# Fetching eight residual tiles one by one inside the down products, behind the LayerNorm transposes

## Chip, cores and metric

One Trainium2 chip, one core of it. The metric is the device time of one execution in microseconds (us). A few other words used below: PE is the matmul engine (TensorE), DVE is VectorE, ACT is ScalarE, POOL is GpSimd, and SP is SyncE, which does no arithmetic here and issues the DMAs in the order of its program.

## The reference

Four layers on `x` of 2048 tokens by 1024 channels in bf16: linear attention (A), a bilinear feed-forward layer (B), and the same two again, each behind a LayerNorm and with a residual.

```python
x = A_x
x = x + _A_ref(_layernorm(x), A_wqkv, A_wo)
x = x + _B_ref(_layernorm(x), B_w_gate, B_w_up, B_w_down)
x = x + _A_ref(_layernorm(x), A_wqkv, A_wo)
x = x + _B_ref(_layernorm(x), B_w_gate, B_w_up, B_w_down)

def _B_ref(x, w_gate, w_up, w_down):          # F = 3584
    g = x @ w_gate ; u = x @ w_up
    return (g * u) @ w_down
```

## The kernel before

Layer B handles its tokens in two halves (`ps_` 0 and 1, 1024 tokens each). Each half has a gate-up stage and a down stage. The down stage is a Strassen-like scheme of seven products, taken in the order 1, 2, 6, 7, 4, 5, 3; the first four have four steps (`t`) of 14 matmuls each. Everything is recorded operation by operation, with the dependences found from byte ranges, and the order in which the program records is the order on each engine. All DMAs but none of the arithmetic go on SP:

```python
def dma(dst_ap, src_ap, wr, key, rd=()):
    P.add("sp", lambda e: e.dma_start(dst_ap, src_ap), rd=rd, wr=wr, dma_sem=key)
```

During the gate-up stage the SBUF space of eight tiles of the residual `x` (128 tokens by 1024, 256 KB each) is lent to scratch. The tiles wait in a DRAM copy (`x_scratch`) and are fetched back when the gate-up stage ends. That is in the last part of its tail, which runs inside the first step of the first down product:

```python
def tail(part):                    # ... parts 0 to 2 end the gate-up stage ...
    for _ in range(2 if "R1" not in order else 1):
        ring_issue()               # weights of the down products, ~0.9 MB each
    for t in range(8 if l2 and not jit else 0):
        i = 8 * ps_ + t
        dma(x_res[:, i, :], xscr[i * 128:(i + 1) * 128, :], r_x(i), KX[i], rd=R(V_X + i * 32, 32))
```

So it happens in three of the four halves; the first half of the first layer lends nothing (`jit`). I call them the first, second and third place. The residual is read where a product is evacuated, that is, read out of PSUM and worked into the output: tiles 0 to 3 of the half first in product 2, tiles 4 to 7 first in product 7:

```python
def evac(t, q=q):                  # after the matmuls of step t of product q
    ...
    elif q in "24":
        xs, rx = xq(sh, 0, t)      # left half of residual tile 4*sh + t
        stt(xs, pb, CD, a, ra_, rx, prd=[bank])
    ...
    ticks(q, t)                    # other work slipped in: LayerNorm steps, stores
    l2_ops(q, t)                   # DVE sums for later products
```

`ticks` carries LayerNorm work. In the second place it is the last four token tiles of this layer's own LayerNorm, needed by the second half. One step hands the previous tile to a DMA transpose on SP, writes the next normalized tile on DVE, and starts the statistics of one more:

```python
def flush_step(self):
    self.step_t(1)                 # SP: dma_start_transpose(xnT[...], xn[n % 2])
    ...
    self.b2_one()                  # DVE: xn[n % 2] = (x - mean) * rstd      (L496)
    ...
    self.start(self.n)             # DVE, POOL: statistics of the next tile
```

For these last tiles there are two buffers `xn`. The write of tile n + 2 has to wait until the transpose of tile n has read its buffer.

## Time and profile before

| | before |
|---|---|
| three runs known to the prediction, median (range), us | 1430.34 (1430.0 to 1430.77) |
| profiled execution, span, us (its device time) | 1429.3 (1431.05) |
| PE busy | 1421.5 us (99 %) |
| DVE busy | 1205.5 us (84 %) |
| second place, from the unbroken row of its first product to the next gate-up stage | 1107.01 to 1186.82 us: 79.81 us |

The prediction shows the page's header, the chain that ended last, and the waits. Two more views of the second place carry the argument. In the timeline of SP (start, length, line, operation, destination<-source, number of DMAs) the eight residual loads stand ahead of the first three transposes, and two weight loads behind those:

```profile
1107.59 4.39 SPq L428 DMA_DIRECT2D arena<-x_scratch  x8
1112.33 10.51 SPq L579 DMA_TRANSPOSE arena<-arena  x3
1122.89 1.06 SPq L428 DMA_DIRECT2D arena<-t_scratch  x2
```

In the timeline of DVE the bracket at the end of a line gives the idle time ahead of it and what ended that:

```profile
1112.57 2.17 DVE L806 TENSOR_TENSOR arena<-arena 128x1792 f16<-128x1792 f16 x2
1121.04 0.55 DVE L496 TENSOR_SCALAR arena<-arena 128x1024 f16<-128x1024 bf16 x1 [6.31 <-DMA arena<-arena]
```

DVE has nothing it may do from 1114.7 to 1121.0, because the buffer that L496 writes is held by the first transpose.

### The profile page before, as it was taken

How to read it: one execution, taken by the hardware profiler on the slowest of the kernel's cores; microseconds unless marked ns; L12 is line 12 of the kernel's file. 1: busy time of each engine (PE TensorE's matmuls, PEld its weight loads, DVE VectorE, ACT ScalarE, POOL GpSimd, SP SyncE). 2: the span in 40 equal slices, each digit the busy share in tenths (PEclk: the TensorE clock that was granted, in tenths of full speed). 3: DMA queues.
4: the chain of work that ended last, by engine and by line, in shares of the span. 5: the costliest groups of instructions: out<-in, count | busy, mean ns of one | idle time of the engine just before them, and what ended most of it. 6: DMA issues, size and time to landing. Idle time of an engine off the chain costs nothing.

```text
span 1429.3 us, 21974 instructions
## 1 busy us (share of the span) xinstructions
PE 1421.5 (99%) x8209; PEld 790.0 (55%) x8209; DVE 1205.5 (84%) x2356; ACT 712.5 (50%) x1455; POOL 154.5 (11%) x193
## 2 busy tenths in 40 slices
PE   9999999999999999999999999999999999999999
PEld 4444444555546566664554444456666475666548
DVE  7897978999888799987689978888888787888888
ACT  5882355444410266655377714567775004777400
POOL 3203521000010000002010045300000100000000
PEclk9999999999999999999999999999999999999999
DMA  7868979997786776769784366767775976777653
GB/s 237 222 142 221 217 177 203 300 316 265 251 263 211 239 255 243 257 222 303 230 280 104 101 173 167 167 197 259 245 255 197 273 255 231 257 263 254 208 194 122
DMA packets 270699, 320.74 MB, mean 224 GB/s; under 512 B 164096, under 2 KB 211072, under 8 KB 270592
## 3 DMA queue, kind: packets, MB, share of 16 engines
q1 hardware_dynamic: 270592, 319.34, 73.1%
q8 instruction: 64, 1.05, 0.3%
q14 instruction: 43, 0.35, 0.1%
HBM read 236.45 MB, written 73.40 MB: 217 GB/s over the span
## 4 chain that ended last, share of the span: by engine, by line
PE 86%; DVE 7%; issue 2%; ACT 2%; POOL 1%; DMA 1%; SPq 0%; POOLq 0%; DVEq 0%
PE ps L1419 28%; PE ps L1502 17%; PE ps L1854 13%; PE ps L1235 8%; PE ps L974 8%; PE ps L1761 6%; PE ps L1337 4%; DVE arena L806 3%; DVE arena L455 2%; PE ps L947 1%; DMA arena<-arena 1%; DVE arena L809 1%; POOL arena L466 1%; PE ps L1261 1%; PE ps L1288 0%
## 5 line engine op out<-in xcount | busy, mean ns | idle before, releaser
L806 DVE TENSOR_TENSOR arena<-arena 128x512 f16<-128x512 f16 (+7 forms) x1027 | 507.2, 522 | 57.2 <-ACT arena L1506 32.7
L1419 PE MATMUL ps<-arena 128*128 128x512 f16 x1888 | 457.1, 379 | 0.5 <-DVE arena L809 0.4
L809 DVE SCALAR_TENSOR_TENSOR arena<-ps,arena 128x512 f16<-128x512 f32 (+3 forms) x558 | 358.4, 658 | 76.8 <-PE ps L1854 36.8
L1502 PE MATMUL ps<-arena 128*128 128x256 f16 x2184 | 287.5, 273 | 0.0
L1419 PEld LDWEIGHTS ps<-arena 128*128 128x128 f16 (+1 forms) x1888 | 182.6, 98 | 163.2 <-ACT ps L1448 3.8
L1502 PEld LDWEIGHTS ps<-arena 128*128 128x128 f16 (+1 forms) x2184 | 211.9, 98 | 90.6 <-ACT arena L1506 6.9
L1854 PE MATMUL ps<-arena 128*128 128x512 bf16 (+1 forms) x1064 | 232.6, 379 | 1.7 <-DVE arena L806 1.7
L1854 PEld LDWEIGHTS ps<-arena 128*128 128x128 f16 x1064 | 103.8, 98 | 125.9 <-DVE arena L806 2.2
L1424 ACT ACTIVATE arena<-ps 128x512 f32<-128x512 f32 x224 | 133.7, 597 | 76.8 <-PE ps L1419 62.9
L1506 ACT ACTIVATE arena<-ps 128x256 f32<-128x256 f32 x351 | 125.1, 384 | 26.4 <-PE ps L1502 21.5
L974 PE MATMUL ps<-arena 128*128 128x512 f16 (+1 forms) x616 | 134.7, 380 | 0.6 <-ACT arena L981 0.6
L1235 PE MATMUL ps<-arena 128*128 128x512 bf16 x512 | 116.1, 379 | 0.0
L1337 PE MATMUL ps<-arena 128*128 128x512 bf16 x512 | 110.8, 379 | 0.0
L1512 ACT COPY ps<-ps 128x256 f32<-128x256 f32 x182 | 66.4, 365 | 75.3 <-DVE arena L809 28.6
L974 PEld LDWEIGHTS ps<-arena 128*128 128x128 f16 x616 | 59.3, 98 | 74.9 <-ACT arena L981 5.8
L1761 PE MATMUL ps<-arena 128*128 128x256 f16 (+1 forms) x882 | 97.2, 273 | 0.5 <-DVE arena L809 0.5
L1448 ACT COPY ps<-ps 128x512 f32<-128x512 f32 x112 | 65.4, 584 | 62.2 <-PE ps L1419 51.9
L1076 POOL TENSOR_TENSOR arena<-arena 128x1024 f16<-128x1024 f32 x32 | 76.2, 2381 | 156.7 <-DVE arena L1074 141.2
L1761 PEld LDWEIGHTS ps<-arena 128*128 128x128 f16 x882 | 86.0, 98 | 11.9 <-DVE arena L809 1.0
L1515 DVE TENSOR_TENSOR ps<-ps,arena 128x256 f32<-128x256 f32 x182 | 76.7, 428 | 10.6 <-PE ps L1502 9.6
L1337 PEld LDWEIGHTS ps<-arena 128*128 128x128 f16 x512 | 50.0, 98 | 60.5
L1789 ACT COPY arena<-ps 128x256 f32<-128x256 f32 x8 | 3.0, 372 | 158.3 <-PE ps L1761 158.3
(72 smaller groups left out, 980.5 us busy)
## 6 DMA issues: line engine op xcount, KB each, us to landing
arena<-w_scratch SPq DMA_DIRECT2D x84, 896.0 KB, 4.5
arena<-t_scratch SPq DMA_DIRECT2D x32, 896.0 KB, 6.0
arena<-in_B_w_down_dram SPq DMA_DIRECT2D x24, 896.0 KB, 5.2
arena<-sp_scratch SPq DMA_DIRECT2D x26, 768.0 KB, 4.2
w_scratch<-arena SPq DMA_DIRECT2D x28, 512.0 KB, 6.2
arena<-w_scratch SPq DMA_DIRECT2D x28, 384.0 KB, 5.1
x_scratch<-arena SPq DMA_DIRECT2D x40, 256.0 KB, 5.0
arena<-x_scratch SPq DMA_DIRECT2D x40, 256.0 KB, 6.1
```

What stands on the lines that cost most here:

```text
L806: P.add("dve", lambda e: e.tensor_tensor(out=out, in0=a, in1=b, op=op), rd=rd, wr=wr, prd=prd)
L809: P.add("dve", lambda e: e.scalar_tensor_tensor(out=out, in0=a, scalar=sc, in1=b, op0=ALU.mult, op1=op1), rd=rd, wr=wr, prd=prd)
L974: P.add("pe", lambda e: [e.matmul(psb(bank), a[0][:, k, :], b[0][:, k, :], start=(q in (1, 5) and k == 0), stop=(k == 3), skip_group_check ...
L1235: return [e.matmul(psb(bank), xrt[t][:, jj * 128:(jj + 1) * 128], pk[:, h, t, :], start=(t == tok[0]), stop=(t == tok[NST - 1])) for t in ts]
L1337: return [e.matmul(psb(bank), xnT[:, g, i * 128:(i + 1) * 128], wp[:, g, dh * 512:(dh + 1) * 512], start=(dh == 0 and g == 0), stop=(g == ...
L1419: P.add("pe", lambda e: [e.matmul(psb(bank), w[:, k, :], x[:, k, :], start=(start and k == 0), stop=(k == 3), skip_group_check=True) for k ...
L1424: P.add("act", lambda e: e.activation(t, psb(bank), AF.Copy, scale=SG), prd=[bank], wr=r)
L1502: P.add("pe", lambda e: [e.matmul(psb(bank)[:, 256 * half:256 * half + 256], w[:, k, :], xx[:, k, :], start=(start and k == 0), stop=(k == ...
L1506: P.add("act", lambda e: e.activation(d, src, AF.Copy, scale=sc), prd=[xk], wr=rd_)
L1515: P.add("dve", lambda e: e.tensor_tensor(out=half(c, 1), in0=U, in1=c5, op=ALU.add), prd=[xk], rd=rc5, pwr=[dst[c]])
L1761: P.add("pe", lambda e: [e.matmul(psb(bank)[:, 256 * half:256 * half + 256], a[:, k, 128 * r:128 * r + 128], b[:, k, :], start=(start and ...
L1854: P.add("pe", lambda e: [e.matmul(psb(bank), hv[:, 7 * hf + k, t * 128:(t + 1) * 128], w[:, k, :], start=(q in "15" and hf == 0 and k == 0 ...
```

## The change

The intent is to take the eight loads from ahead of the transposes and give each to a step one or two products ahead of its use: tiles 0 to 3 behind the `ticks` of product 1 (used in product 2), tiles 4 to 7 behind those of product 2 (used in product 7, the fourth).

```diff
                     for _ in range(2 if "R1" not in order else 1):
                         ring_issue()
-                    for t in range(8 if l2 and not jit else 0):
-                        i = 8 * ps_ + t
-                        dma(x_res[:, i, :], xscr[i * 128:(i + 1) * 128, :], r_x(i), KX[i], rd=R(V_X + i * 32, 32))
                 return tail
@@ evac @@
                         ticks(q, t)
+                        if q in "12" and (ps_ or not first):
+                            i = i0 + 4 * "12".index(q) + t
+                            dma(x_res[:, i, :], xscr[i * 128:(i + 1) * 128, :], r_x(i), KX[i], rd=R(V_X + i * 32, 32))
                         l2_ops(q, t)
```

## The prediction

> **What bounds the kernel now.** I read the page's header, then the chain that ended last, then the waits and the engines' timelines of the one stretch the chain pointed to.
>
> ```profile
> span 1429.3 us, 21974 instructions
> PE 1421.5 (99%) x8209; PEld 790.0 (55%) x8209; DVE 1205.5 (84%) x2356; ACT 712.5 (50%) x1455; POOL 154.5 (11%) x193
> ```
>
> TensorE (PE) is busy for all but 1429.3 - 1421.5 = 7.8 us. That is a hint only, since the ends of matmuls are modelled, so I take the pitch of matmuls from unbroken rows of the chain: 259 of 128x512 in 55.90 us are 0.2158 us each, 196 of 128x256 in 21.40 us are 0.1092 us each. Where matmuls follow each other at this pitch, no moved transfer can gain anything. The change touches three places, the heads of three of the four down stages, near 649, 1107 and 1351 us. Of the first and the third the chain says:
>
> ```profile
> 648.85 55.90 PE ps L1854 x259
> 704.75 21.40 PE ps L1761 x196
> ...
> 1350.65 43.81 PE ps L1854 x203
> 1394.46 29.82 PE ps L1761 x273
> ```
>
> The columns are start and length. Both places run at the pitch without a break (203 x 0.2158 = 43.8; 273 x 0.1092 = 29.8): nothing is to be had there. At the second, which is the first down stage of the second bilinear layer, the chain leaves PE and goes through the DMA queue:
>
> ```profile
> 1106.29 0.90 PE ps L1419 x4
> ...
> 1107.59 0.43 SPq L428
> ...
> 1111.54 0.44 SPq L428
> 1111.98 0.35 issue
> 1112.33 8.61 DMA arena<-arena
> ```
>
> The L428 rows from 1107.59 to 1111.98 are the issues of the eight residual loads (256 KB each). The last row is the first LayerNorm transpose, an SBUF-to-SBUF DMA that stood behind them and took 8.61 us to land; the median over the 60 transposes of this line is 4.0 us. The waits of this stretch say who paid:
>
> ```profile
> DVE arena L496 <- DMA arena<-arena: 6.3, 1, 6.3
> ...
> PE ps L1854 <- DVE arena L806: 1.7, 1, 1.7
> ...
> PE ps L1761 <- DVE arena L809: 0.5, 1, 0.5
> ```
>
> VectorE (DVE) stood still once, 6.3 us, because its next LayerNorm output (L496) writes one of two buffers and the late transpose was still reading that one. From there DVE works with a backlog, and later PE waits for DVE twice. The timeline of PE shows where:
>
> ```profile
> 1107.01 31.89 PE L1854 MATMUL ps<-arena 128*128 128x512 bf16 x147
> 1140.57 12.26 PE L1854 MATMUL ps<-arena 128*128 128x512 f16 x56 [1.66 <-DVE arena L806]
> 1152.66 3.98 PE L1761 MATMUL ps<-arena 128*128 128x256 f16 x35
> 1157.15 17.75 PE L1761 MATMUL ps<-arena 128*128 128x256 f16 x161 [0.50 <-DVE arena L809]
> ```
>
> Start to start: 147 x 0.2158 = 31.73, so the fourth product could start at 1138.74 and starts at 1140.57: 1.83 us lost. 56 x 0.2158 leads to 1152.66, as seen. 35 x 0.1092 = 3.82 leads to 1156.48, and the next starts at 1157.15: 0.67 us lost. Together 2.50 us in this stage; after 1157.15 the rows join again.
>
> **What the Trainium skill says.** (1) "DMA: Bandwidth & Descriptors", section "Queues, rings and completion order": on each DMA engine descriptors are consumed in ring order, and SP owns one row of rings. All these transfers are issued from SP, so bytes issued earlier are moved earlier; the 8.61 us against 4.0 agree. (2) The same page, "Anatomy of one DMA": DMA engines do not wait on semaphores, the issuing sequencer does, before it dispatches. So one blocked issue on SP holds all that follow. The queue's own waits in this stretch agree: it waits 3.3 and 3.9 us ahead of two transposes whose source DVE had not written, and the two weight loads behind them went out only at 1122.89. (3) "TensorE: Matmul & The Clock Gate", section "Wait — 56ns, not 53.3ns?": back-to-back matmuls of N = 512 are 215.7 ns apart once warm. The trace has 215.8 and a granted clock of 1.000: PE has no slack of its own.
>
> **The change part by part.** It removes the block of eight residual loads at the end of the gate-up stage's tail (three places, 24 loads) and issues the same 24 one at a time: tiles 0 to 3 behind the four steps of the first down product, tiles 4 to 7 behind those of the second. No instruction is added or dropped on any compute engine: built, both kernels have the same 734 and 1737 rows of PE and DVE work, in the same order. Bytes moved stay the same. Only SP's order changes. In the second place it becomes transpose, load, transpose, load, transpose, load, two weight loads, transpose, load, and so on.
>
> *Transpose.* The eight issues took 4.39 us, and 8 x 0.262 = 2.1 MB at the roughly 390 GB/s that the DMA view gives there take about 5.4 us. The first transpose can now go out at about 1107.6 instead of 1112.33, with only a 0.92 MB weight load (2.4 us) ahead of it. At its usual 4 us it lands by about 1113 to 1115.
>
> *DVE.* Before the wait DVE was done with its other work at 1112.57 + 2.17 = 1114.74, and L496 began at 1121.04. So the 6.3 us shrink to 0 to 1, and DVE is 5.3 to 6.3 us earlier on everything after it that it is not waiting for PE with.
>
> *PE.* At 1140.57 PE needed DVE 1.83 us earlier: covered 3 times over. At the second loss PE now comes 1.83 us sooner (1154.65) and DVE must be 2.5 us earlier than it was. DVE gets there the last evacuation of the fourth product at PE's 1138.74 + 12.09 = 1150.83, then about 0.7 + 1.1 + 3 x 0.35 = 2.9 us of its own work: 1153.7, about 1 us in time. So both losses go: 2.5 us.
>
> *Residual loads.* The one question is whether they come too late. In the second place tile 0 is needed at DVE's first evacuation of the second product, 1128.30 before, about 1122 now; issued by about 1108 it lands (median 6.1 us) by 1115. Tile 3 goes out behind the fourth transpose and is wanted at about 1130; if the queue keeps step that is 5 us or more after its landing. Tiles 4 to 7 are first read in the fourth product, over 12 us after their issue. In the first place tile 3 stands behind a store and three 512 KB loads that take 8.5 us to land: it may come 1 to 2 us late for DVE at 668.5. But DVE idles 0.3 to 1.3 us ahead of each evacuation there and makes that up, and the PSUM bank it empties is not needed again until two products later. In the third place the loads wait for outputs of the same step, with 10 us in hand.
>
> Sum: 1430.34 - 2.5 + 0 + 0 = 1427.84, say 1427.8 us.
>
> **The rivals.** (a) *A wait takes the place of the one removed.* SP blocks on a transpose whose source DVE has not written, and the residual tile or weight load behind it is late; DVE then waits in the second product instead. For it: the queue is in order, and the weight load at 1122.89 was already just in time (PE's weight path waited 0.2 us for it). Against it: with DVE and transposes early, those weight loads go out near 1117, and each residual tile has 5 us or more. It would leave 0 to 1 us of gain: 1429.3 to 1430.3. (b) *The transpose stays slow anyway.* DMA share is 1.02 of the engines in this stretch, so the transpose could owe its 8.6 us to traffic of any kind. For it: two transposes of the first place took long too. Against it: 2.1 MB of the 3.0 MB ahead of it are the residual tiles. If half the delay stays, DVE still gains 3 us, enough for the first loss but hardly the second: 1428.5. (c) *More than 2.5.* A DVE that is 5 us ahead could also drop short waits of the gate-up stage that follows. But of the 16 waits of the weight path there, 0.3 us each, 15 are for ScalarE (ACT) and one is for DVE: half a microsecond at most, 1427.3. (d) *The first or third place gets a new PE wait.* Nothing in the timelines is nearer than some 10 us of slack to PE; it would add 0.5 to 2 us.
>
> **Range and chances.** Runs of the kernel before lie within 0.8 us. The full effect gives 1427.8 give or take 0.4, rivals (a), (b) and (d) pull upward to 1429.5, (c) downward: eight times in ten 1427.0 to 1429.3. Two per cent are 28.6 us. PE's whole idle time is 7.8 us, so faster by that much is not possible; slower by that much would need a stall that nothing shows. Chances 0.005, 0.985 and 0.01.
>
> **What would show it.** In the changed trace: the first transpose near 1107.6 lands in 4 to 7 us; the 6.3 us wait of L496 is under 1 us; the rows of PE from 1107 to 1175 have no gap over 0.2 us, so the x161 row begins about 2.5 us earlier; the gate-up stage that follows begins near 1184.5 instead of 1186.98; the first and third places keep their unbroken rows of 55.9 and 43.8 us. I am wrong if DVE waits in the second product for an `x_scratch` load, if PE's gap only moves to another product, or if the times before 1107 differ by more than 0.5 us, which would mean that the first place matters.

## The result

| | before | changed |
|---|---|---|
| median (range), us, 4 runs each | 1430.55 (1430.0 to 1430.96) | 1428.51 (1428.3 to 1428.78) |
| profiled execution, span, us | 1429.3 | 1427.0 |
| second place, us | 79.81 | 1107.18 to 1184.48: 77.30 |
| DVE's wait for the transpose | 6.31 us | none |

The ratio is 0.9986, with a 95 % interval of 0.9969 to 1.0003: by the total alone not even clear of nothing. A ratio here is the mean time of one kernel's fast runs over the mean of the other's in the same rounds, so it is not quite the ratio of the medians in the table. What makes the gain certain is the place where it occurs. Here is SP's timeline of the changed kernel in the second place:

```profile
1107.76 1.24 SPq L579 DMA_TRANSPOSE arena<-arena  x1
1109.04 0.75 SPq L428 DMA_DIRECT2D arena<-x_scratch  x1
...
1117.84 0.91 SPq L428 DMA_DIRECT2D arena<-t_scratch  x2
```

The first transpose goes out 4.6 us earlier and lands 6.8 us after its issue, at 1114.5; the two weight loads go out 5 us earlier. DVE now waits only for POOL's reciprocal square root of the variance (L466):

```profile
1112.73 2.16 DVE L806 TENSOR_TENSOR arena<-arena 128x1792 f16<-128x1792 f16 x2
1115.36 0.55 DVE L496 TENSOR_SCALAR arena<-arena 128x1024 f16<-128x1024 bf16 x1 [0.46 <-POOL arena L466]
```

And PE's timeline, which had two breaks here, has none: its rows follow at the pitch of the prediction. (Of 203 matmuls two records are missing, and the line numbers are three lower because of the edit.)

```profile
1107.18 43.98 PE L1851 MATMUL ps<-arena 128*128 128x512 bf16 x201
1150.99 21.56 PE L1758 MATMUL ps<-arena 128*128 128x256 f16 x196
1172.61 12.03 PE L1851 MATMUL ps<-arena 128*128 128x512 bf16 x54
1184.48 5.78 PE L1419 MATMUL ps<-arena 128*128 128x512 f16 x26
```

The account of the two profiled spans closes: the stage is 2.51 us shorter, it began 0.17 us later (1107.18 against 1107.01), and from the next gate-up stage to the end it took 0.04 us longer (242.52 against 242.48). Sum -2.30 us, and the spans are 1429.3 and 1427.0.

The change made one new wait, in the first place, which the waits of that stretch show. (Of its 1.65 us DVE had idled 1.21 us there before too, for PE.)

```profile
DVE arena L809 <- DMA arena<-x_scratch: 1.6, 1, 1.6
```

### The profile page after: what moved, and what is told of

Its sections match the earlier page's. It is cut to its first block, busy times and chain, and to the rows that moved or that the text cites. A ratio compares the mean times of both kernels' runs of the same rounds, so it can differ in the third digit from the quotient of the medians.

```text
span 1427.0 us, 21915 instructions
## 1 busy us (share of the span) xinstructions
PE 1418.2 (99%) x8150; PEld 791.5 (55%) x8209; DVE 1205.3 (84%) x2356; ACT 713.0 (50%) x1455; POOL 155.9 (11%) x193
## 4 chain that ended last, share of the span: by engine, by line
PE 90%; DVE 5%; ACT 2%; issue 1%; DMA 1%; POOL 0%; SPq 0%; DVEq 0%
PE ps L1419 28%; PE ps L1502 17%; PE ps L1851 16%; PE ps L1235 8%; PE ps L974 8%; PE ps L1337 6%; PE ps L1758 5%; DVE arena L806 2%; DVE arena L455 1%; PE ps L947 1%; DVE arena L809 1%; ACT arena L666 1%; DMA arena<-in_A_wqkv_dram 1%; PE ps L1261 1%; PE ps L1288 0%
```

## The experiments

My theory: the whole gain comes from the second place. The transpose lands late there because of what stands ahead of it; it holds a buffer; DVE waits and then runs late; PE loses what of DVE's lateness exceeds DVE's slack. Rivals: spreading the 24 loads is what helps, wherever it happens; the traffic slows the transpose wherever it is issued from; the late weight loads are the cause; the new wait in the first place eats part of the gain.

Total times scatter by half a microsecond or more, and even the moment at which the second place begins moves between 1106.65 and 1107.93 us from profile to profile. The length of the second place, from the start of PE's unbroken row to the start of the next gate-up stage, is much steadier, so I give both. Each chip had its own nine runs of the kernel before (medians 1430.38, 1430.88 and 1430.78).

| run | median, us | before, us | DVE's wait for a transpose, us | second place, us |
|---|---|---|---|---|
| kernel before | 1430.55 | | 6.31 | 79.81 |
| changed kernel | 1428.51 | 1430.55 | none | 77.30 |
| second place only | 1428.95 | 1430.38 | none | 77.30 |
| first and third only | 1430.48 | 1430.38 | 5.48 | 78.98 |
| block behind the first transpose | 1429.32 | 1430.38 | 2.12 | 77.30 |
| four ahead | 1428.63 | 1430.38 | 1.3 | 77.30 |
| seven ahead | 1431.73 | 1430.78 | 7.02 | 80.51 |
| sixteen ahead | 1435.38 | 1430.88 | 10.18 | 83.88 |
| spare buffers | 1428.87 | 1430.88 | none | 77.30 |
| block on ACT's queue | 1431.09 | 1430.88 | 6.2 | 79.64 |
| the same, one step later | 1428.88 | 1430.78 | 3.03 | 77.30 |
| small loads ahead | 1428.92 | 1430.88 | none | 77.30 |
| tile 3 earlier (first place) | 1428.62 | 1430.78 | none | 77.30 |

### Which place: the second only, and the first and third only

```diff
-                        if q in "12" and (ps_ or not first):
+                        if q in "12" and not first and not ps_:    # second only; elsewhere the block stays
```

> Only the second place (the down stage near 1107 us) has the new order; the first and third keep the block of eight. Theory (the gain is the late transpose in the second place and nothing else): 2.0 to 2.6 us under the kernel before, as with the whole change; VectorE's 6.3 us wait for the transpose is gone and PE's rows from 1107 to 1175 join without a gap. Rival (spreading 24 loads in three places is what helps): about a third of the gain, 0.7 us.

```diff
-                        if q in "12" and (ps_ or not first):
+                        if q in "12" and ps_:                      # first and third; in the second the block stays
```

> The first and third places have the new order, the second keeps the block of eight ahead of the transposes. Theory: the time of the kernel before within 0.3 us; the 6.3 us wait and PE's losses of 1.83 and 0.67 us are there again, and the 1.6 us wait of VectorE for a residual tile in the first place (seen in the changed kernel) is there and costs nothing. Rival (spreading): two thirds of the gain, about 1.4 us.

With the second place alone the stage takes 77.30 us, and the total is 1.4 us under the kernel before (ratio 0.9990, interval 0.9977 to 1.0002), which is less than expected. With the other two alone the total is that of the kernel before (ratio 1.0000, interval 0.9988 to 1.0013) and PE's two breaks are back:

```profile
1139.99 12.26 PE L1854 MATMUL ps<-arena 128*128 128x512 f16 x56 [0.83 <-DVE arena L806]
...
1156.57 17.75 PE L1761 MATMUL ps<-arena 128*128 128x256 f16 x161 [0.50 <-DVE arena L809]
```

Spreading as such is out: the gain is in the second place. But note the size. With the same block of eight ahead of the transposes, DVE waited 5.48 us in this execution and not 6.31, and the stage lost 1.68 us against 77.30 and not 2.51. The loss is not a constant of the program.

### What stands ahead: the block behind the first transpose, and four ahead

```diff
                         ticks(q, t)
-                        if q in "12" and (ps_ or not first):
+                        for k in range(8 if q == "1" and t == 0 and not first and not ps_ else 0):
+                            i = i0 + k
+                            dma(x_res[:, i, :], ...)               # all eight, behind the first transpose
+                        if q in "12" and ps_:
```

> As the changed kernel, but in the second place all eight loads go out in one block straight behind the first transpose. Theory (only what stands ahead of the first transpose matters): the whole gain within 0.5 us, 1428.2 to 1428.9; the first transpose lands in about 6 us; the second, now behind 2.1 MB, is late by some 3 us, so VectorE waits 0 to 3 us one step later, under the 3.3 us it has to spare, and PE has no gap over 0.3 us. Rival (spreading): the time of the kernel before.

```diff
+                    for t in range(4 if not first and ps_ == 0 else 0):   # in the tail
+                        dma(x_res[:, 8 * ps_ + t, :], ...)
...
-                        if q in "12" and (ps_ or not first):
+                        if q in ("12" if ps_ else "" if first else "2"):
```

> As the changed kernel, but in the second place tiles 0 to 3 are issued in a block ahead of the first transpose, tiles 4 to 7 one by one under the second product. Theory with a threshold: half the issues and bytes ahead give VectorE a wait of 2 to 4 us instead of 6.3; VectorE has about 3.3 us to spare (it came 5.85 us sooner in the changed kernel and PE got back 2.5), so PE loses 0 to 0.5 us: 1428.2 to 1429.0. Rival (the loss of PE is in proportion to the bytes ahead): half the gain, 1.1 to 1.25 us.

The block of eight directly behind the first transpose costs the stage nothing: 77.30 us. The first transpose landed in 6.1 us; the second, now behind the block, took 7.9, and DVE waited 2.12 us for it one step later. So it is what stands ahead that matters. Spreading the loads over two products is not needed, although the total of this run (1429.32) is the highest of those with 77.30 us, and above the 1428.2 to 1428.9 expected; its profiled execution was late already when the second place began (1107.93). Four ahead gave a smaller wait than I had expected (1.3 us against 2 to 4), and no loss. A wait of up to 3.03 us (the run "one step later" below) is free.

### Dose: sixteen ahead and seven ahead

```diff
-                    for t in range(8 if l2 and not jit else 0):
+                    for t in (list(range(8)) * (1 if ps_ else 2) if l2 and not jit else ()):   # from the kernel before
```

> The kernel before, with the block of eight in the second place issued twice over (the same data again, so the result stays right; each second load waits for the first of its tile). Theory (one for one above a threshold: PE's loss in the stage is VectorE's wait for the transpose less 3.8 us, as 6.31 gave 2.51 and 5.5 gave 1.68): the wait grows to 11 to 15 us, the stage loses 7 to 11 us against its floor of 77.30, the time is 1435 to 1439. The two weight loads behind the transposes are late as well by then, so part of PE's wait may bear the name of a weight load. Rival (proportion to the bytes ahead): 5 us lost, 1433.

```diff
+                    for t in range(7 if not first and ps_ == 0 else 0):   # in the tail
...
-                        if q in "12" and (ps_ or not first):
+                        if q in "12" and (ps_ or not first and (q, t) == ("2", 3)):
```

> As the changed kernel, but in the second place seven tiles are issued in a block ahead of the first transpose and the eighth under the second product. Theory with a threshold: four ahead gave VectorE a wait of 1.3 us, eight gave 5.5 and 6.3, so seven give 4.3 to 5.2; PE's loss is the wait less 3.8 us, 0.5 to 1.4 us over the floor of 77.30, the time 1429.0 to 1430.0. Rival (a step: either all is lost or nothing): a loss of 0 or 2.5 us.

The runs with seven, eight and eight ahead, and the one on ACT's queue, have waits of 7.02, 6.31, 5.48 and 6.2 us and losses (length less 77.30) of 3.21, 2.51, 1.68 and 2.34. In each the loss is the wait less 3.8 us, to within 0.1 us, and the runs with waits of 3.03 us and less have no loss. One for one above a threshold holds for these. (With seven, 0.43 us of the loss fell a product earlier, at a late weight load.) What failed is my estimate of the wait from the number of loads: seven made it 7.02, more than either profile of eight. The transpose took 9.9 us to land there, against 8.6 and 7.9. The total missed its range as well. The five timed runs of that kernel lie between 1429.8 and 1432.17, so it varies from execution to execution. Why, no run shows.

The run with sixteen fits the same line by its numbers (10.18 - 3.8 = 6.4, loss 6.58), but its trace says otherwise. (Wait and loss both stayed just under what was expected.) PE did not wait for DVE at all. The weight loads behind the transposes went out only at 1127.27, and PE stood still for one of them. DVE's lateness is behind this too: the third transpose, ahead of the weight loads in SP's queue, waits for what L496 writes, so they go out 1.85 us after L496 begins (1125.42), just as in the kernel before (1121.04 and 1122.89). The first two lines below are from PE's timeline; the others, from the view by windows, give for each stretch its length, then busy time and number of instructions of PE, PEld (PE's weight loads), DVE, ACT and POOL, then PE's granted clock, the DMA share and GB/s:

```profile
1107.53 21.32 PE L1854 MATMUL ps<-arena 128*128 128x512 bf16 x96
1132.44 25.65 PE L1854 MATMUL ps<-arena 128*128 128x512 f16 x105 [3.59 <-DMA arena<-t_scratch]
```

```profile
1128.60:1132.40 3.80, 0.25 (x2) 0.00 (x0) 3.31 (x4) 0.00 (x0) 1.39 (x1) 0.86 0.96 326
...
1134.00:1136.00 2.00, 2.00 (x6) 0.76 (x5) 2.00 (x4) 0.00 (x0) 0.00 (x0) 0.50 1.19 297
1136.00:1138.00 2.00, 2.00 (x7) 0.65 (x5) 2.00 (x3) 0.00 (x0) 0.00 (x0) 0.50 0.59 214
1138.00:1140.00 2.00, 2.00 (x10) 0.89 (x9) 2.00 (x3) 0.00 (x0) 0.00 (x0) 0.96 0.25 83
```

The gap is 1132.44 - 1107.53 - 98 x 0.2158 = 3.76 us, with the two missing records counted. From about 1131.4, inside the gap, until about 1138.2 PE's clock was granted at half (0.50; the two turns follow from the means 0.86 and 0.96 of the first and last stretch), and the 105 matmuls that follow the gap took 1157.93 - 1132.44 = 25.49 us instead of 22.66, another 2.83 us. 3.76 + 2.83 = 6.59. So this run confirms that more ahead costs more, and shows a second path by which it does (DVE late, so weights late, and a halved clock behind them). It is no evidence for the one-for-one rule; that the numbers agree is chance.

### The link between transpose and DVE: spare buffers

This is the kernel before, with the block of eight ahead everywhere, but the last two normalized tiles of the second layer B get buffers of their own, in scratch that is free until product 7.

```diff
                 o = (O_XN + [O_WQ])[n % 3] if self.to == "B" and n < 14 else O_XN[n % 2]
+                if self.spare and n >= 14:                    # set for the second layer B
+                    o = O_R + (n - 14) * 2048
                 return vh(o, D), R(o, D * 2)
...             # their transposes get semaphores of their own
```

> The kernel before with its block of eight ahead of the transposes in all places, but the last two LayerNorm tiles of the second bilinear layer get output buffers of their own (scratch of the later products), so VectorE need not wait for the late transposes. Theory (the late transpose hurts only through the buffer that it holds): VectorE's wait on the transposes is gone though the first transpose still lands 7 to 9 us after its issue, the stage takes 77.3 to 77.6 us, and the gain is 2.0 to 2.6 us. Rival (the late transposes or the traffic hurt in another way as well, through the weight load of the third product or through the transposed data itself): less than 1 us of gain, with PE or VectorE waiting for a DMA.

The first transpose still landed late (7.9 us), DVE did not wait, and the stage took 77.30 us. The total gains 2.0 us (1428.87 against 1430.88, ratio 0.9986, interval 0.9973 to 0.9998). So the late transpose hurts through the buffer it holds and through nothing else: not through the transposed data, and not through the traffic. The late weight loads went out 2.8 us earlier in this run as well (1120.09), but they are not the cause in the kernel before: there PE's weight path waited 0.2 us for one and PE itself not at all.

### Issue time or bytes: small loads ahead

The changed kernel, with eight loads of 64 columns each put ahead of the first transpose in the second place. The full loads follow as in the changed kernel, so the result is right.

```diff
+                    for t in range(8 if not first and ps_ == 0 else 0):   # in the tail
+                        dma(x_res[:, t, 0:64], xscr[t * 128:(t + 1) * 128, 0:64], r_x(t, 0, 64), KX[t], rd=R(V_X + t * 32, 32))
```

> As the changed kernel, but in the second place eight small loads (64 columns of each tile, a sixteenth of the bytes) stand ahead of the first transpose, as many issues as in the kernel before; the full loads follow as in the changed kernel. It separates the time of issuing from that of moving. Theory (both count): the transpose goes out near 1111.5 to 1112.3 as before but lands in 4 to 5 us, VectorE waits 1 to 2 us instead of 6.3, so issue time makes up 1 to 2 us of the wait and the bytes the rest; PE loses nothing: 1428.2 to 1429.0. Rival (the issue time is the whole of it): a wait of 4 us or more.

The eight issues took 3.75 us, the transpose went out at 1112.15, nearly as late as in the kernel before, and landed 3.4 us later, at 1115.55. DVE came to L496 at 1115.66, held up only by POOL's 0.46 us. Even the 1 to 2 us that I expected are not there. The time that SP needs to issue eight loads is free here by itself; with a sixteenth of the bytes there is no wait at all.

### Another queue: ACT issues the loads

As "block behind the first transpose", but issued by ACT, in the first step and in another run in the second. SP's queue then has nothing between the transposes.

```diff
+                        for k in range(8 if q == "1" and t == 0 and not first and not ps_ else 0):   # t == 1 in the later run
+                            i = i0 + k
+                            P.add("act", lambda e, i=i: e.dma_start(x_res[:, i, :], xscr[i * 128:(i + 1) * 128, :]),
+                                  rd=R(V_X + i * 32, 32), wr=r_x(i), dma_sem=KX[i])
```

> As the changed kernel, but in the second place the eight loads go out in one block at the same time as in the kernel before, issued by ScalarE instead of SP, so the traffic is the same but the transposes do not stand behind it in SP's queue. Theory (place in SP's issue order and rings): the first transpose goes out near 1107.5 and lands in 4 to 8 us, VectorE waits under 2.5 us, no loss of PE: 1428.2 to 1429.0. Rival (2.1 MB of traffic at that time slows the transpose wherever it was issued): the wait is 4 us or more and the gain 1 us or less.

> As the run with ScalarE issuing the block in the second place, but one step later, so that the first transpose is issued some 2 us ahead of the first of these loads. In the earlier run the transpose, issued 1.3 us behind the first load, took 13.2 us to land. Theory (two queues share the DMA engines, and the transpose gets the small share whatever was issued first): it still takes 8 us or more, VectorE waits 1.5 us or more for it, more than for the same block behind the transpose in SP's own queue (no wait for the first transpose). Rival (only bytes issued ahead of it count, in whichever queue): it lands in under 7 us and VectorE does not wait for it.

The first of these broke the theory in the form I had given it. The transpose went out at 1107.23 with only a weight load ahead of it in its own queue, and took longer from issue to landing than in any other run, as the chain of waits shows:

```profile
1107.23 13.21 DMA arena<-arena
```

DVE waited 6.2 us, the stage lost 2.34 us, and the time was that of the kernel before. ACT had issued the first residual load at 1105.96, 1.3 us ahead of the transpose, and the last by 1110.3, so five of the eight went out after it. (ACT also began 0.7 us ahead of the stage, where SP in the kernel before began 0.6 us into it; the timing is not quite the same.) The rival (traffic slows it wherever it is issued) is right here. In the later run ACT's loads began at 1108.67. The first transpose, issued at 1107.53, landed in 6.8 us as in the changed kernel, so my expectation of 8 us or more was wrong for it. The second, issued at 1111.04 in the middle of ACT's loads, took 11.2 us, and DVE waited 3.03 us for it. In SP's own queue a transpose straight behind the same 2.1 MB took 7.9 to 8.6 us, but these figures leave out the 4.2 to 4.6 us in which SP had issued the loads first. Counted from the start of the stage, the first transpose landed after 13.8 us with ACT's loads and after 13.9 us in the kernel before; the second, after 15.3 us in the later run and after 14.4 us behind SP's block. So bytes under way in another queue hold a transpose up about as much as bytes ahead of it in its own, or somewhat more; and loads that SP issues behind it do not (6.1 us). "Its place in SP's queue" was too narrow. What these runs show is that SP's loads do no harm when they are issued behind the transpose, and that ACT's do none to a transpose issued 1.1 us ahead of the first of them. How the DMA engines share their time between the two queues was not measured.

### The new wait in the first place

```diff
+                        early = q == "1" and t == 3 and first and ps_ == 1
+                        if not early:
+                            ticks(q, t)
                         if q in "12" and (ps_ or not first):
                             ...                                # the residual load
+                        if early:
+                            ticks(q, t)
```

> The changed kernel, but in the first place residual tile 3 is issued ahead of the LayerNorm store and the three 512 KB weight loads of its step. Theory (VectorE's 1.6 us wait for that tile lies inside its own slack): the wait is gone and the time is that of the changed kernel, 1428.2 to 1429.0. Rival (that wait is what keeps the changed kernel from gaining the whole 2.5 us): 0.5 us faster than the changed kernel or more.

DVE's wait for the tile is gone, and the median is 1428.62 against 1428.51 of the changed kernel: no difference that could be read. The wait lay inside DVE's slack.

No run points to a version that beats the changed kernel: the second place stands at 77.30 us in eight different kernels, which is its matmuls at PE's pitch (259 x 0.2158 + 196 x 0.1092 = 77.3), and the first and third places had no loss to begin with.

## Why the prediction was right

The predicted time was 1427.8 us in a range of 1427.0 to 1429.3; the measured median is 1428.51.

- *Nothing to gain in the first and third place.* Shown: the run with only these two has the time of the kernel before. In the changed kernel the rows there start at 648.85 and 1348.15 and are unbroken.
- *The transpose lands by 1113 to 1115.* It landed at 1114.5, 6.8 us after its issue. The working gave it 2.4 us behind a weight load and 4 us of its own, 6.4.
- *DVE is 5.3 to 6.3 us earlier.* It was 5.85 us earlier relative to the stage's start: its first evacuation of product 2 began at 1122.62, against 1128.30, with the start 0.17 us later. The spare buffers show that this is the link.
- *Both of PE's losses go, 2.5 us.* Right for the profiled executions, to 0.01 us. The margin at the second loss, put at about 1 us, also holds: DVE finished at 1152.80 + 1.08 = 1153.88 what PE needed at 1150.99 + 3.82 = 1154.81.
- *The size in the median.* The median gained 2.04 us, not 2.5, and this is the term that was mis-sized. I took the loss from one execution, and a slow one: the profiled execution of the kernel before took 1431.05 us, more than any of the four timed runs beside it (1430.0 to 1430.96). The loss depends on when a transpose lands among other traffic, and that varies: two profiles with the same block ahead in the second place lost 2.51 and 1.68 us. Their mean of 2.1 is close to the 2.04 of the medians and the 2.01 of the spare buffers. With two profiles this is a reason, not a proof. The rest of the 0.67 us by which the predicted time was low is the fourth run, which raised the median of the kernel before by 0.21 us.
- *Tile 3 of the first place 1 to 2 us late, without cost.* The lateness was put too high: DVE's step began at 669.13 against 668.53, with the stage 0.16 us later, so the tile was 0.44 us late. The other 1.21 us of the wait of 1.65 us DVE had spent waiting for PE before. At the next evacuation it had caught up, and taking the wait away changed nothing.
- *Rivals.* (a), a new wait in the second product of the second place, did not come: DVE waits for no residual tile there. (b), the traffic slows the transpose anyway, is wrong for the change as made, because the loads come behind the transpose; but the run with ACT's queue shows that the concern was real. What the prediction drew from the ring order, that "bytes issued earlier are moved earlier", fits the runs within SP's queue (6.1 us with the block behind the transpose) but not across two queues. The queue also blocked on transposes as (a) feared (2.4 to 3.0 us at each of three), but the weight loads went out at 1117.84, near the 1117 of the working. (c) and (d) did not come: the rest of the run from the next gate-up stage on differs by 0.04 us.

## What to carry to other kernels

When a trace shows one engine waiting for a small DMA, look at what was issued just ahead of it and when each of those bytes is first read; fetch late what is needed late, and put the small transfer with the nearer deadline first. Moving the bulk loads to another issuing engine's queue is no substitute: the small transfer was as late, or later, until the loads also began after it. Measure a gain of less than two tenths of a per cent inside its stage, where it shows as 2.51 us of 79.81, rather than in the total, and take more than one profile of the stage before putting a number on it.

## What the Trainium skill lacked or had wrong

- "DMA: Bandwidth & Descriptors", "DMA Transpose (X-bar)": no time to landing for one SBUF-to-SBUF transpose of 128x1024 in fp16. The runs show 3.4 us with little ahead of it, 5.8 to 6.8 behind a 0.9 MB load, 7.9 to 9.9 behind some 2 MB in its own queue, 11.2 and 13.2 while 2.1 MB from another queue were under way.
- The same page, "Issuing engines are not separate DMA queues": it says that DMAs of different engines interleave, and that issuing from several only saves the sequencer's time; it gives no figure for what the interleaving costs a small transfer. The runs show a cost: with the loads issued by ACT, five of the eight after the transpose, it took 13.2 us, and with the same loads behind it in SP's queue 6.1.
- The same page, "Specifications": an HBM limit of about 358 GB/s for a core. The row is a stack's rate divided by two cores, so it is no ceiling when one core is at work: the kernel before moved 396 GB/s from 1112.3 to 1116 us, mostly residual tiles from DRAM.
- "TensorE: Matmul & The Clock Gate", "What's actually happening": at least one window of about 3.4 us idle for the half clock and one of about 3.4 us of work for the full one, the windows running freely. Neither time can be planned with as it stands. In the run with sixteen loads ahead the half clock came about 2.5 us after PE's last work (1128.85 to about 1131.4), sooner than a whole idle window, and the full clock about 5.7 us after work had resumed (1132.4 to about 1138.2). The 6.8 us at half clock between are about two windows.
